# Two interleaved attention layers on one core: P transposed over 80 columns, P.V in whole-array matmuls, the row load moved into mid-step, the local layer's weights loaded in step one, and shorter last steps

## The chip, the cores and the metric

The kernel runs on one core of one Trainium2 chip. The metric is device time in microseconds (us) of one execution; lower is better. Engines are named as the profile names them: PE (matmuls), PEld (loads of the stationary operand into PE), DVE (vector), ACT (scalar), POOL (GpSimd) and SP (which here only issues DMAs; its queue is SPq).

## What is computed

Two layers, A and B, are applied one after the other, and then both again to the result. `x` has 2048 rows of 640 features.

```python
x = x + A(layernorm(x)); x = x + B(layernorm(x))
x = x + A(layernorm(x)); x = x + B(layernorm(x))

def A(x):                                   # 32 heads of 192, segments of 32 rows
    mem = mem0                              # 8 rows
    for s in range(64):
        h = concat([mem, x[32*s:32*s + 32]])          # 40 rows
        q, k, v = h @ Wq, h @ Wk, h @ Wv              # per head
        p = softmax(where(mask, q @ k.T / sqrt(192), -1e9))
        o = (p @ v) @ Wo
        mem, out_s = o[:8], o[8:]                     # memory goes on to the next segment

def B(x):                                   # 32 heads of 20, window of 8 keys, every second row back
    q, k, v = split(x @ wqkv)
    attn = softmax(where(pos - 2*w >= 0, q . k[pos - 2*w] / sqrt(20), -1e9))
    return (sum_w attn * v[pos - 2*w]) @ wo
```

In layer A each segment needs the memory of the segment before it, so the segments follow one another.

## The kernel before

**Steps.** The two passes run together. In step s, layer A works on segment s of the first pass (l = 0) and on segment s - 2 of the second (l = 1): 2 x 40 = 80 rows that share each weight. The local layer B works one step behind on the same two passes. There are 67 steps, 0 to 66: layer A runs in steps 0 to 65, layer B in steps 1 to 66. In steps 65 and 66 nothing is left of the first pass for layer B, and before the change its half is computed all the same.

**Weights.** Layer A's weights come in 64 pieces of 480 KB, called halves: 32 for q and k, 16 for v, 16 for the output. 31 stay in SBUF. The other 33 are streamed again in every step through a ring of 5 buffers (`half`, L216): in step 0 from the inputs, with a copy laid out for later written to DRAM by POOL's queue (L227), and from step 1 on from that copy (L230), in two DMAs of 240 KB, 66 in a step. All are issued by SP in the order in which PE uses the halves, and one is issued only when the half that had its buffer five loads earlier has been used.

**The order within a step** is written out by hand in `ORDER` (L53): each word is a call. PE and SP keep exactly this order (`manual_schedule`, L532); for DVE, ACT and POOL a scheduler decides the order when the program is built, and each engine then runs its own list in that order.

- `q` i (L295): q and k of two heads in 60 matmuls of 80 columns; ACT copies the result (L310).
- `v` i (L339): v of two heads in 5 matmuls of 384 columns; DVE copies the odd ones (L362), ACT the even ones (L360), into vt.
- `s` g (L312): scores of a group of 8 heads: 16 matmuls on 64x64 tiles of the array and 16 on 128x64 tiles. On DVE: mask (L330), maximum (L332), subtraction (L333); the exponential on ACT (L334); then on DVE sum (L336), reciprocal (L337) and product (L338), which gives P, the tile Pm.
- `t` g (L341): four transposes of Pm on PE (L345); DVE and ACT copy one half of the partitions each into PT (L347, L348).
- `pv` g (L365): P.V of the group on 128x64 tiles: 24 matmuls (L373), two tiles at a time; ACT copies the result (L376).
- `o` j (L379): the output projection, added up over the whole step in two accumulators (L390).
- For layer B: `ln1` (L418), `qkv` (L424; the products of q and k on DVE for l = 0 and on POOL for l = 1, L445), `logits` (L448, on 128x32 tiles; its softmax L465 to L473 ends with attn), `e` c (L477: PE spreads attn, DVE multiplies, L483, and adds up, L485), `wo` (L487) and `ln2` (L505).

At the end of a step `finish_step` (L393) has DVE copy the new memory into the next step's input (ST, L401); the next `q0` waits for it.

**Rows of x.** Every four steps 128 rows are loaded (`input_load`, L239), normalized on DVE and ACT (bst L249, L250, lnst, xn L254) and transposed by PE (`input_tile`, L243). The load is issued as steps 1, 5, 9, ... begin (L549), the transposes stand at `input0` in the step after. `store` (L512) writes 128 finished rows every four steps.

**Local weights.** wqkv (2400 KB) and wo (800 KB) are loaded whole as step 0 begins, ahead of all halves (L545).

Of the kernel before, what the change touches and what calls it, by code (L numbers as in the profile page):

```python
# [45 lines left out]
LAG = 2  # L46
# [4 lines left out]


ORDER = """  # L53
q0 v0 q1 ln10 alpha0 q2 v1 input0 q3 v2 s0 q4 qkv0 v3 t0 q5 q6 v4 q7 v5 logits0
s1 pv0 q8 o0 o1 v6 q9 e0 t1 v7 q10 o2 o3 e1 q11 v8
s2 pv1 q12 e2 o4 o5 v9 q13 e3 t2 v10 o6 o7 q14 e4 v11 q15 v12
s3 pv2 wo0 o8 v13 v14 ln20 t3 v15 store0 o9 o10 pv3 o11 o12 o13 o14
"""


def stages():

    names = ("alpha", "ln1", "qkv", "logits", "input", "wo", "ln2", "store", "pv", "q", "s", "t", "v", "o", "e")
# [43 lines left out]
class Kernel:  # L107
# [108 lines left out]
    def half(self, h):  # L216
# [123 lines left out]

    def p_transpose(self, g):  # L341
        nc = self.nc
        ps = self.ps.tile([P, 4, 2, SLOT], BF16, name="pt_ps", tag="ps")
        for j in range(4):
            nc.tensor.transpose(out=ps[:, j, :, :].rearrange("p h q -> p (h q)"),  # L345
                                in_=self.Pm[g % 2][:, j, :, :].rearrange("p l t -> p (l t)"), identity=self.ident[:, :])
        nc.vector.tensor_copy(out=self.PT[g % 2][0:64, :, :, 0, :], in_=ps[0:64, :, :, 0:LT])  # L347
        nc.scalar.copy(out=self.PT[g % 2][64:128, :, :, 1, :], in_=ps[64:128, :, :, 0:LT])  # L348

    def v(self, i):  # L350
        nc = self.nc
# [10 lines left out]
            nc.vector.tensor_copy(out=vt[:, :], in_=ps[:, :])  # L362
        self.vts[i] = vt

    def pv(self, g):  # L365
        nc = self.nc
        for k in (2 * g, 2 * g + 1):
            ps = self.ps.tile([P, 2, 3, 2, LT], F32, name="o_ps", tag="ps")
            for jj in range(2):
                i = 2 * k + jj  # L370
                vt = self.vts.pop(i)
                for (n, slot, h, col) in ((0, 0, 0, 0), (0, 1, 0, 64), (1, 0, 0, 128), (1, 1, 1, 192), (2, 0, 1, 256), (2, 1, 1, 320)):
                    nc.tensor.matmul(ps[64 * slot:64 * (slot + 1), jj, n, :, :], lhsT=vt[:, col:col + 64], rhs=self.PT[g % 2][:, i % 4, h, :, :],  # L373
                                     start=True, stop=True, tile_position=(0, 64 * slot))
# [40 lines left out]
        self.xr_next = xr  # L415


    def b_stats(self):  # L418
        self.bs = self.ln_stats(self.xr[:, :, :, :].rearrange("p c l t -> p c (l t)"), 2 * SEG)
        xn = self.w1.tile([P, NCH, 2 * SEG], BF16, name="xnB", tag="n")  # L420
        self.ln_apply(self.xr[:, :, :, :].rearrange("p c l t -> p c (l t)"), *self.bs, xn[:, :, :], 2 * SEG)
        self.xnB = xn

    def b_qkv(self):  # L424
        nc = self.nc
        qT = self.w1.tile([P, NCH, 2, SEG], BF16, name="qT", tag="q")
        kh = self.w2.tile([P, NCH, 2, BPAD + SEG], BF16, name="kh")
        vh = self.w2.tile([P, NCH, 2, BPAD + SEG], BF16, name="vh")
        for new, old in ((kh, self.kh), (vh, self.vh)):
            if old is None:  # L430
                nc.gpsimd.memset(new[:, :, :, 0:BPAD], 0.0)
            else:
                nc.gpsimd.tensor_copy(out=new[:, :, :, 0:BPAD], in_=old[:, :, :, SEG:SEG + BPAD])
        for kind, dst in enumerate((qT[:, :, :, :], kh[:, :, :, BPAD:], vh[:, :, :, BPAD:])):
            ps = self.ps.tile([P, NCH, 2, SEG], F32, name="qkv_ps", tag="ps")
            for d in range(NCH):
                for c in range(NCH):
                    nc.tensor.matmul(ps[:, d, :, :], lhsT=self.wqkv[:, c, kind * D + d * P:kind * D + (d + 1) * P],  # L438
                                     rhs=self.xnB[:, c, :].rearrange("p (l t) -> p l t", l=2), start=(c == 0), stop=(c == NCH - 1))
            nc.scalar.copy(out=dst, in_=ps[:, :, :, :])  # L440
        self.qT, self.kh, self.vh = qT, kh, vh
        self.prod = self.w1.tile([P, NCH, 2, BW, SEG], BF16, name="prod")
        for l in range(2):
            eng = nc.vector if l == 0 else nc.gpsimd
            eng.tensor_tensor(out=self.prod[:, :, l, :, :], in0=qT[:, :, l, :].unsqueeze(2).to_broadcast([P, NCH, BW, SEG]),  # L445
                              in1=window(kh, l), op=ALU.mult)

    def b_logits(self):  # L448
        nc = self.nc
        hf = SEG // 2  # L450
        ps = self.ps.tile([P, BW, hf], F32, name="lg_ps", tag="ps")
# [24 lines left out]

    def b_expand(self, c):  # L477
        nc = self.nc
        ps = self.ps.tile([P, 2, BW, SEG], F32, name="bc_ps", tag="ps")
        nc.tensor.matmul(ps[:, :, :, :].rearrange("p l w t -> p (l w t)"), lhsT=self.ET[:, c, :],  # L480
                         rhs=self.attn[:, :, :, :, :].rearrange("p l w h t -> p (l w h t)"), start=True, stop=True)
        pv = self.prod[:, c, :, :, :]
        nc.vector.tensor_tensor(out=pv, in0=ps[:, :, :, :], in1=window1(self.vh, c), op=ALU.mult)  # L483
        with nc.allow_low_precision("bf16 result of an f32 sum"):
            nc.vector.tensor_reduce(out=self.oT[:, c, :].rearrange("p (l t) -> p l t", l=2), in_=pv.rearrange("p l w t -> p l t w"), op=ALU.add, axis=AX.X)  # L485

    def b_wo(self):  # L487
        nc, s = self.nc, self.step
        ps = self.ps.tile([P, NCH, 2, SEG], F32, name="y_ps", tag="ps")
        for d in range(NCH):  # L490
            for c in range(NCH):
                nc.tensor.matmul(ps[:, d, :, :].rearrange("p l t -> p (l t)"), lhsT=self.wo[:, c, d * P:(d + 1) * P], rhs=self.oT[:, c, :],  # L492
                                 start=(c == 0), stop=(c == NCH - 1))
        if s <= self.n_seg:
            x2 = self.w2.tile([P, NCH, SEG], BF16, name="x2")
# [29 lines left out]
    def run(self):  # L525
# [6 lines left out]
        with tc.manual_schedule(engines={PE, SP}):  # L532
# [86 lines left out]
```

## Time and profile before

| | |
|---|---|
| Median of 3 runs | 3517.87 us (3513.82 to 3522.08) |
| The profiled execution | 3520.67 us, its span 3519.0 us |
| DVE, ACT, POOL busy | 62%, 42%, 11% of the span |
| Step 0 (first q0 matmul to that of step 1) | 128.9 us |
| Steps 4 to 61, mean by s mod 4 = 0, 1, 2, 3 | 52.22, 50.62, 51.83, 51.09 us |
| From the last q0 (step 65, at 3438.3) to the end | 80.7 us |
| Read from DRAM, written | 1091.7 MB, 18.8 MB |

The profile's page gives busy times and what each group of instructions waited for. The costliest groups on the lines that the change touches (line, engine, operation, output from input, shapes, count; then busy time and the mean of one; then idle time just before, and what ended it):

```profile
L373 PE MATMUL o_ps<-PT,vt 128*64 128x80 bf16 x6336 | 161.1, 203 | 0.5 <-issue 0.4
L345 PE MATMUL pt_ps<-ident,Pm 128*128 128x128 bf16 x1056 | 103.6, 221 | 0.6 <-issue 0.3 <-DVE Pm L338 0.2
L347 DVE COPY PT<-pt_ps 64x320 bf16<-64x320 bf16 x264 | 80.7, 306 | 15.0 <-PE pt_ps L345 15.0
L485 DVE TENSOR_REDUCE oT<-prod 128x64 bf16<-128x512 bf16 x330 | 336.7, 1021 | 4.5
```

A matmul's duration of some 200 ns is its latency: many are under way at once. What one costs in a stream is read from the distance between the starts, or from the chain of waits. The timeline gives start and length of each instruction, with equal neighbours merged (x15), and for an engine that stood idle, for how long and what ended it.

### The profile page before, as it was taken

How to read it: one execution, taken by the hardware profiler on the slowest of the kernel's cores; microseconds unless marked ns; L12 is line 12 of the kernel's file. 1: busy time of each engine (PE TensorE's matmuls, PEld its weight loads, DVE VectorE, ACT ScalarE, POOL GpSimd, SP SyncE). 2: the span in 40 equal slices, each digit the busy share in tenths (PEclk: the TensorE clock that was granted, in tenths of full speed). 3: DMA queues.
4: the chain of work that ended last, by engine and by line, in shares of the span. 5: the costliest groups of instructions: out<-in, count | busy, mean ns of one | idle time of the engine just before them, and what ended most of it. 6: DMA issues, size and time to landing. Idle time of an engine off the chain costs nothing.

```text
span 3519.0 us, 172521 instructions
## 1 busy us (share of the span) xinstructions
PE 3388.8 (96%) x78044; PEld 2891.7 (82%) x78045; DVE 2197.2 (62%) x5056; ACT 1479.6 (42%) x3213; POOL 369.9 (11%) x467
## 2 busy tenths in 40 slices
PE   5799999999999999999999999999999999999997
PEld 3588888888888888888888888888888888888886
DVE  1366666666666666666666666666666666666665
ACT  1244444444444444444444444444444444444443
POOL 2110110010111011001101101110010111011000
PEclk7799999999999999999999999999999999999998
DMA  9999999999999999999999999999999999999995
GB/s 350 352 321 320 318 320 315 316 320 323 319 323 317 317 314 322 320 322 319 322 326 322 324 322 320 318 324 326 321 319 323 315 320 324 320 317 319 319 320 202
DMA packets 664961, 1121.84 MB, mean 319 GB/s; under 512 B 70744, under 2 KB 661472, under 8 KB 664224
## 3 DMA queue, kind: packets, MB, share of 16 engines
q1 hardware_dynamic: 659280, 1091.96, 92.5%
q0 software_dynamic: 2640, 16.22, 1.1%
q8 instruction: 610, 9.99, 1.1%
q10 hardware_dynamic: 2304, 2.62, 0.2%
q14 instruction: 127, 1.04, 0.1%
HBM read 1091.68 MB, written 18.84 MB: 316 GB/s over the span
## 4 chain that ended last, share of the span: by engine, by line
PE 83%; DMA 9%; DVE 4%; ACT 2%; SPq 1%; issue 1%; ACTq 0%; POOLq 0%; POOL 0%; DVEq 0%
PE qk_ps L308 29%; PE v_ps L356 21%; PE acc L390 13%; DMA wt<-Wr 4%; PE qkv_ps L438 4%; PE o_ps L373 3%; PE s_ps L326 3%; PE s_ps L320 3%; PE qk_ps L303 2%; PE bc_ps L480 2%; DMA x_sb<-in_A_x_dram 2%; PE pt_ps L345 1%; DMA wt<-in_A_Wv_dram 1%; SPq L214 1%; PE y_ps L492 1%
## 5 line engine op out<-in xcount | busy, mean ns | idle before, releaser
L310 ACT CAST QK<-qk_ps 128x480 bf16<-128x480 f32 x1056 | 581.5, 557 | 1042.7 <-PE qk_ps L308 828.5
L356 PE MATMUL v_ps<-wt,ST 128*128 128x384 bf16 x3630 | 717.4, 328 | 13.9 <-DMA wt<-in_A_Wv_dram 9.2
L308 PE MATMUL qk_ps<-ST,wt 128*128 128x80 bf16 x14850 | 687.8, 203 | 22.6 <-DMA wt<-in_A_Wq_dram 10.6
L308 PE MATMUL qk_ps<-ST,res 128*128 128x80 bf16 x14850 | 691.4, 202 | 18.1 <-DMA res<-in_A_Wq_dram 9.4
L308 PEld LDWEIGHTS <-wt 128*128 128x128 bf16 x14850 | 610.1, 100 | 78.8 <-DMA wt<-in_A_Wq_dram 11.8
L356 PEld LDWEIGHTS <-ST 128*128 128x128 bf16 x5280 | 466.1, 99 | 246.6 <-issue 16.4
L308 PEld LDWEIGHTS <-res 128*128 128x128 bf16 x14850 | 610.9, 100 | 48.9 <-DMA res<-in_A_Wq_dram 10.4
L390 PE MATMUL acc<-ot,res 128*128 128x80 bf16 x9900 | 465.6, 202 | 17.4 <-DMA res<-in_A_Wo_dram 9.6
L390 PEld LDWEIGHTS <-res 128*128 128x128 bf16 x9900 | 409.9, 100 | 38.3 <-DMA res<-in_A_Wo_dram 11.8
L362 DVE CAST vt<-v_ps 128x384 bf16<-128x384 f32 x528 | 290.2, 550 | 210.0 <-PE v_ps L356 209.8
L483 DVE TENSOR_TENSOR prod<-bc_ps,vh 128x512 bf16<-128x512 f32 x330 | 227.3, 689 | 245.0 <-PE bc_ps L480 244.4
L360 ACT CAST vt<-v_ps 128x384 bf16<-128x384 f32 x528 | 253.7, 481 | 244.8 <-PE v_ps L356 243.2
L485 DVE TENSOR_REDUCE oT<-prod 128x64 bf16<-128x512 bf16 x330 | 336.7, 1021 | 4.5
L356 PE MATMUL v_ps<-res,ST 128*128 128x384 bf16 x1650 | 326.8, 329 | 2.7 <-DMA res<-in_A_Wv_dram 2.7
L390 PE MATMUL acc<-ot,wt 128*128 128x80 bf16 x5940 | 309.9, 202 | 6.2 <-DMA wt<-in_A_Wo_dram 3.5
L376 ACT CAST ot<-o_ps 128x480 bf16<-128x480 f32 x528 | 268.4, 559 | 109.3 <-PE o_ps L373 109.3
L330 DVE TENSOR_TENSOR sb<-s_ps,maskA 128x320 f32<-128x320 f32 x264 | 129.7, 491 | 253.7 <-PE s_ps L326 253.6
L390 PEld LDWEIGHTS <-wt 128*128 128x128 bf16 x5940 | 261.3, 100 | 18.1 <-issue 4.7
L445 POOL TENSOR_TENSOR prod<-qT,kh 128x1280 bf16<-128x1280 bf16 x66 | 169.9, 2575 | 653.0 <-ACT kh L440 653.0
L348 ACT COPY PT<-pt_ps 64x320 bf16<-64x320 bf16 x264 | 110.9, 420 | 296.7 <-DVE PT L347 295.1
L273 POOL TENSOR_TENSOR sq<-x 128x160 f32<-128x160 bf16 x64 | 28.9, 452 | 1837.4 <-DVE x L496 1837.4
L445 DVE TENSOR_TENSOR prod<-qT,kh 128x1280 bf16<-128x1280 bf16 x66 | 201.2, 3048 | 3.4 <-ACT kh L440 3.4
(117 smaller groups left out, 3709.3 us busy)
## 6 DMA issues: line engine op xcount, KB each, us to landing
wt<-Wr SPq DMA_DIRECT2D x4290, 240.0 KB, 4.8
Wr<-wt POOLq DMA_DIRECT2D x33, 480.0 KB, 6.7
wt<-in_A_Wv_dram SPq DMA_DIRECT2D x11, 480.0 KB, 10.5
res<-in_A_Wo_dram SPq DMA_DIRECT2D x10, 480.0 KB, 10.8
wt<-in_A_Wk_dram SPq DMA_DIRECT2D x9, 480.0 KB, 11.1
res<-in_A_Wq_dram SPq DMA_DIRECT2D x9, 480.0 KB, 11.3
res<-in_A_Wk_dram SPq DMA_DIRECT2D x7, 480.0 KB, 10.2
wt<-in_A_Wq_dram SPq DMA_DIRECT2D x7, 480.0 KB, 10.2
```

The lines of the kernel that those rows point to most:

```text
L308: nc.tensor.matmul(ps[:, m, :, :], lhsT=w[m // 3][:, c, (m % 3) * P:(m % 3 + 1) * P], rhs=st[:, c, :, 0:LT], start=(c == 0), stop=(c == NC ...
L310: nc.scalar.copy(out=self.QK[i % NQK][:, 0:12 * LT], in_=ps[:, :, :, :].rearrange("p m l t -> p (m l t)"))
L330: nc.vector.tensor_tensor(out=sb[:, :, :], in0=sv, in1=self.maskA[:, :].unsqueeze(1).to_broadcast([P, 8, LT]), op=ALU.add)
L356: nc.tensor.matmul(ps[:, :], lhsT=st[:, c, :, :].rearrange("p l t -> p (l t)"), rhs=w[:, c, :], start=(c == 0), stop=(c == NCH - 1))
L360: nc.scalar.copy(out=vt[:, :], in_=ps[:, :])
L362: nc.vector.tensor_copy(out=vt[:, :], in_=ps[:, :])
L376: nc.scalar.copy(out=ot[:, :, :, :], in_=ps[:, :, :, :, :].rearrange("p j n l t -> p (j n) l t"))
L390: nc.tensor.matmul(a[:, at, :, :], lhsT=w[h][:, m, dc * P:(dc + 1) * P], rhs=self.ots[h // 2][:, 3 * (h % 2) + m, :, :], start=(h == 0 and ...
L438: nc.tensor.matmul(ps[:, d, :, :], lhsT=self.wqkv[:, c, kind * D + d * P:kind * D + (d + 1) * P], rhs=self.xnB[:, c, :].rearrange("p (l t) ...
L445: eng.tensor_tensor(out=self.prod[:, :, l, :, :], in0=qT[:, :, l, :].unsqueeze(2).to_broadcast([P, NCH, BW, SEG]), in1=window(kh, l), op=A ...
L483: nc.vector.tensor_tensor(out=pv, in0=ps[:, :, :, :], in1=window1(self.vh, c), op=ALU.mult)
L485: nc.vector.tensor_reduce(out=self.oT[:, c, :].rearrange("p (l t) -> p l t", l=2), in_=pv.rearrange("p l w t -> p l t w"), op=ALU.add, axi ...
```

## The change

- P is transposed by an ordinary matmul with the identity matrix, of which only the 80 columns that are used are moved; the result is float32 in PSUM.
- P.V is in two calls. `pm` (pv_main) does features 0 to 127 of the first head and the last 128 columns for the second in whole-array matmuls of 128 features, 8 in a group; `pt` (pv_tail) does the remaining 64 features of each head on 128x64 tiles, 8 in a group. In groups 0 to 2 `pm` stands ahead of the next group's scores and `pt` behind them.
- The row load is a word of its own, `load0`, after `t0` in steps 2, 6, 10, ..., and `input0` stands after `v9` of the same step.
- wqkv and wo are loaded in step 1, in five chunks each, ahead of q0 to q4 and of q8 to q12.
- In steps 65 and 66 layer B computes the second pass alone; in step 66 the product that POOL had is done by DVE.

```diff
-q0 v0 q1 ln10 alpha0 q2 v1 input0 q3 v2 s0 q4 qkv0 v3 t0 q5 q6 v4 q7 v5 logits0
-s1 pv0 q8 o0 o1 v6 q9 e0 t1 v7 q10 o2 o3 e1 q11 v8
-s2 pv1 q12 e2 o4 o5 v9 q13 e3 t2 v10 o6 o7 q14 e4 v11 q15 v12
-s3 pv2 wo0 o8 v13 v14 ln20 t3 v15 store0 o9 o10 pv3 o11 o12 o13 o14
+q0 v0 q1 ln10 alpha0 q2 v1 q3 v2 s0 q4 qkv0 v3 t0 load0 q5 q6 v4 q7 v5 logits0
+pm0 s1 pt0 q8 o0 o1 v6 q9 e0 t1 v7 q10 o2 o3 e1 q11 v8
+pm1 s2 pt1 q12 e2 o4 o5 v9 input0 q13 e3 t2 v10 o6 o7 q14 e4 v11 q15 v12
+pm2 s3 pt2 wo0 o8 v13 v14 ln20 t3 v15 store0 o9 o10 pm3 pt3 o11 o12 o13 o14
...
+    def local_weights(self, i):
+
+        if i < NCH:
+            self.nc.sync.dma_start(out=self.wqkv[:, i, :], in_=self.B_wqkv[i * P:(i + 1) * P, :])
+        elif 8 <= i < 8 + NCH:
+            self.nc.sync.dma_start(out=self.wo[:, i - 8, :], in_=self.B_wo[(i - 8) * P:(i - 7) * P, :])
...
     def p_transpose(self, g):
-        ps = self.ps.tile([P, 4, 2, SLOT], BF16, name="pt_ps", tag="ps")
+        ps = self.ps.tile([P, 4, 2, LT], F32, name="pt_ps", tag="ps")
         for j in range(4):
-            nc.tensor.transpose(out=ps[:, j, :, :].rearrange("p h q -> p (h q)"),
-                                in_=self.Pm[g % 2][:, j, :, :].rearrange("p l t -> p (l t)"), identity=self.ident[:, :])
+            nc.tensor.matmul(ps[:, j, :, :], lhsT=self.Pm[g % 2][:, j, :, :].rearrange("p l t -> p (l t)"), rhs=self.ident[:, :].rearrange("p (h t) -> p h t", h=2)[:, :, 0:LT],
+                             start=True, stop=True)
...
-    def pv(self, g):
+    def pv_main(self, g):
+        self.ops = []
         for k in (2 * g, 2 * g + 1):
             ps = self.ps.tile([P, 2, 3, 2, LT], F32, name="o_ps", tag="ps")
             for jj in range(2):
                 i = 2 * k + jj
-                vt = self.vts.pop(i)
-                for (n, slot, h, col) in ((0, 0, 0, 0), (0, 1, 0, 64), (1, 0, 0, 128), (1, 1, 1, 192), (2, 0, 1, 256), (2, 1, 1, 320)):
-                    nc.tensor.matmul(ps[64 * slot:64 * (slot + 1), jj, n, :, :], lhsT=vt[:, col:col + 64], rhs=self.PT[g % 2][:, i % 4, h, :, :],
-                                     start=True, stop=True, tile_position=(0, 64 * slot))
+                for n, h in ((0, 0), (2, 1)):
+                    nc.tensor.matmul(ps[:, jj, n, :, :], lhsT=self.vts[i][:, P * n:P * (n + 1)], rhs=self.PT[g % 2][:, i % 4, h, :, :],
+                                     start=True, stop=True)
+            self.ops.append(ps)
+
+    def pv_tail(self, g):
+        for k, ps in zip((2 * g, 2 * g + 1), self.ops):
+            for jj in range(2):
+                i = 2 * k + jj
+                vt = self.vts.pop(i)
+                for h in range(2):
+                    hs = slice(SLOT * h, SLOT * (h + 1))
+                    nc.tensor.matmul(ps[hs, jj, 1, :, :], lhsT=vt[:, P + SLOT * h:P + SLOT * (h + 1)], rhs=self.PT[g % 2][:, i % 4, h, :, :],
+                                     start=True, stop=True, tile_position=(0, SLOT * h))
...
+    def layers(self):
+
+        return (0, 1) if self.step <= self.n_seg else (1,)
...
-        for l in range(2):
-            eng = nc.vector if l == 0 else nc.gpsimd
+        for l in self.layers():
+            eng = nc.vector if l == 0 or self.step > self.n_seg + LAG - 1 else nc.gpsimd
...
     def b_expand(self, c):
+        ls = slice(self.layers()[0], 2)
...
-        nc.tensor.matmul(ps[:, :, :, :].rearrange("p l w t -> p (l w t)"), lhsT=self.ET[:, c, :],
-                         rhs=self.attn[:, :, :, :, :].rearrange("p l w h t -> p (l w h t)"), start=True, stop=True)
+        nc.tensor.matmul(ps[:, ls, :, :].rearrange("p l w t -> p (l w t)"), lhsT=self.ET[:, c, :],
+                         rhs=self.attn[:, ls, :, :, :].rearrange("p l w h t -> p (l w h t)"), start=True, stop=True)
...
-                if s == 0:
-                    nc.sync.dma_start(out=self.wqkv[:], in_=self.B_wqkv.rearrange("(c p) n -> p c n", p=P))
-                    nc.sync.dma_start(out=self.wo[:], in_=self.B_wo.rearrange("(c p) n -> p c n", p=P))
                 self.x2 = self.x2_next
-                if s % 4 == 1 and 4 * (s // 4 + 1) < self.n_seg:
-                    self.input_load(s // 4 + 1)
                 for what, i in PLAN:
+                    if s == 1 and what == "q":
+                        self.local_weights(i)
...
+                    elif what == "load" and s % 4 == 2 and 4 * (s // 4 + 1) < self.n_seg:
+                        self.input_load(s // 4 + 1)
                     elif what == "input" and s % 4 == 2 and 4 * (s // 4 + 1) < self.n_seg:
                         self.input_tile(s // 4 + 1)
```

More of the change, by code (lines that the diff above doesn't have):

```diff
@@ L53 @@
 ORDER = """
-q0 v0 q1 ln10 alpha0 q2 v1 input0 q3 v2 s0 q4 qkv0 v3 t0 q5 q6 v4 q7 v5 logits0
-s1 pv0 q8 o0 o1 v6 q9 e0 t1 v7 q10 o2 o3 e1 q11 v8
-s2 pv1 q12 e2 o4 o5 v9 q13 e3 t2 v10 o6 o7 q14 e4 v11 q15 v12
-s3 pv2 wo0 o8 v13 v14 ln20 t3 v15 store0 o9 o10 pv3 o11 o12 o13 o14
+q0 v0 q1 ln10 alpha0 q2 v1 q3 v2 s0 q4 qkv0 v3 t0 load0 q5 q6 v4 q7 v5 logits0
+pm0 s1 pt0 q8 o0 o1 v6 q9 e0 t1 v7 q10 o2 o3 e1 q11 v8
+pm1 s2 pt1 q12 e2 o4 o5 v9 input0 q13 e3 t2 v10 o6 o7 q14 e4 v11 q15 v12
+pm2 s3 pt2 wo0 o8 v13 v14 ln20 t3 v15 store0 o9 o10 pm3 pt3 o11 o12 o13 o14
 """
 def stages():
-    names = ("alpha", "ln1", "qkv", "logits", "input", "wo", "ln2", "store", "pv", "q", "s", "t", "v", "o", "e")
+    names = ("alpha", "ln1", "qkv", "logits", "load", "input", "wo", "ln2", "store", "pm", "pt", "q", "s", "t", "v", "o", "e")
     plan = []
@@ L342, in p_transpose @@
         nc = self.nc
-        ps = self.ps.tile([P, 4, 2, SLOT], BF16, name="pt_ps", tag="ps")
+        ps = self.ps.tile([P, 4, 2, LT], F32, name="pt_ps", tag="ps")
         for j in range(4):
-            nc.tensor.transpose(out=ps[:, j, :, :].rearrange("p h q -> p (h q)"),
-                                in_=self.Pm[g % 2][:, j, :, :].rearrange("p l t -> p (l t)"), identity=self.ident[:, :])
-        nc.vector.tensor_copy(out=self.PT[g % 2][0:64, :, :, 0, :], in_=ps[0:64, :, :, 0:LT])
-        nc.scalar.copy(out=self.PT[g % 2][64:128, :, :, 1, :], in_=ps[64:128, :, :, 0:LT])
+            nc.tensor.matmul(ps[:, j, :, :], lhsT=self.Pm[g % 2][:, j, :, :].rearrange("p l t -> p (l t)"), rhs=self.ident[:, :].rearrange("p (h t) -> p h t", h=2)[:, :, 0:LT],
+                             start=True, stop=True)
+        nc.vector.tensor_copy(out=self.PT[g % 2][0:64, :, :, 0, :], in_=ps[0:64, :, :, :])
+        nc.scalar.copy(out=self.PT[g % 2][64:128, :, :, 1, :], in_=ps[64:128, :, :, :])
     def v(self, i):
@@ L453, in b_logits @@
             for r in range(4):
-                nc.tensor.matmul(ps[32 * r:32 * (r + 1), :, :], lhsT=self.E[:, c, :], rhs=self.prod[:, c, r // 2, :, hf * (r % 2):hf * (r % 2 + 1)],
+                nc.tensor.matmul(ps[32 * r:32 * (r + 1), :, :], lhsT=self.E[:, c, :], rhs=self.prod[:, c, max(r // 2, self.layers()[0]), :, hf * (r % 2):hf * (r % 2 + 1)],
                                  start=(c == 0), stop=(c == NCH - 1), tile_position=(0, 32 * r))
@@ L478, in b_expand @@
         nc = self.nc
+        ls = slice(self.layers()[0], 2)
         ps = self.ps.tile([P, 2, BW, SEG], F32, name="bc_ps", tag="ps")
[L480 to L483 removed]
+        nc.tensor.matmul(ps[:, ls, :, :].rearrange("p l w t -> p (l w t)"), lhsT=self.ET[:, c, :],
+                         rhs=self.attn[:, ls, :, :, :].rearrange("p l w h t -> p (l w h t)"), start=True, stop=True)
+        pv = self.prod[:, c, ls, :, :]
+        nc.vector.tensor_tensor(out=pv, in0=ps[:, ls, :, :], in1=window1(self.vh, c, ls), op=ALU.mult)
         with nc.allow_low_precision("bf16 result of an f32 sum"):
[L485 removed]
+            nc.vector.tensor_reduce(out=self.oT[:, c, :].rearrange("p (l t) -> p l t", l=2)[:, ls, :], in_=pv.rearrange("p l w t -> p l t w"), op=ALU.add, axis=AX.X)
     def b_wo(self):
         nc, s = self.nc, self.step
+        ls = slice(self.layers()[0], 2)
         ps = self.ps.tile([P, NCH, 2, SEG], F32, name="y_ps", tag="ps")
@@ L491, in b_wo @@
             for c in range(NCH):
-                nc.tensor.matmul(ps[:, d, :, :].rearrange("p l t -> p (l t)"), lhsT=self.wo[:, c, d * P:(d + 1) * P], rhs=self.oT[:, c, :],
+                nc.tensor.matmul(ps[:, d, ls, :].rearrange("p l t -> p (l t)"), lhsT=self.wo[:, c, d * P:(d + 1) * P], rhs=self.oT[:, c, SEG * ls.start:],
                                  start=(c == 0), stop=(c == NCH - 1))
@@ L537, in run @@
             n_steps = self.n_seg + LAG
-            attend = {"q": self.qk, "s": self.scores, "t": self.p_transpose, "v": self.v, "pv": self.pv, "o": self.o}
+            attend = {"q": self.qk, "s": self.scores, "t": self.p_transpose, "v": self.v, "pm": self.pv_main, "pt": self.pv_tail, "o": self.o}
             local = {"ln1": self.b_stats, "qkv": self.b_qkv, "logits": self.b_logits, "wo": self.b_wo, "ln2": self.beta_x, "store": self.store}
```

5 lines of the change are left out of this document (3 added, 2 removed).

## Prediction

> **What bounds the kernel now.** I read the page's busy times and granted clock first, then the chain of waits and the timeline of step 45 (2410.25 to 2460.47 us, the first q0 matmul of one step to that of the next), then the waits by releaser.
>
> ```profile
> PE 3388.8 (96%) x78044; PEld 2891.7 (82%) x78045; DVE 2197.2 (62%) x5056; ACT 1479.6 (42%) x3213; POOL 369.9 (11%) x467
> PEclk7799999999999999999999999999999999999998
> ```
>
> PE is busy 96% of the span at full clock outside step 0. In the chain (start, length in us) nearly every piece of step 45 is PE work:
>
> ```profile
> 2427.92 0.36 PE s_ps L320 x16
> 2428.28 0.36 PE s_ps L326 x16
> 2428.64 0.44 PE o_ps L373 x24
> 2429.08 1.18 PE qk_ps L308 x30
> ...
> 2433.44 0.22 PE pt_ps L345 x4
> ```
>
> A step with no stall takes 50.2 us (step 45); the mean of steps 8 to 59 is 51.44. Of the 1.22 above the floor, 0.21 is work that only every fourth step has (row and output transposes, 0.56 + 0.28), 0.25 the wait shown last below, and about 0.76, 49 us in all, short waits for streamed weights. So PE is first, the weight stream is close behind (DMA share 0.97 in step 45), and what makes PE wait counts in full.
>
> **Transposes.** 4 in 0.22 us, 56 ns each at 128 columns; 80-column matmuls take 36 ns each (30 in 1.07). The change saves 264 x 4 x 20 ns = 21.1 us. The product now comes out in float32: DVE's copy PT (306 ns, L347) has no such row; a plain bf16 copy is the low end, the 128x384 float32 cast (550, L362) scaled to 320 elements the high one, 0.46. I take 0.46, as it too casts from PSUM; it is hidden, since pm3, the tightest, runs 1.5 us after t3 and the copies need 1.1.
>
> **P.V.** 24 half-array matmuls, run in pairs, take 0.44, or 36.7 ns a pair. Per head pair three such pairs become two whole matmuls (36) and one pair: 4 x 108 ns = 0.43. Nothing is gained. The price of changing the array's shape is in the row after o_ps: 1.18 instead of 1.07, 0.1 us. Groups 1 to 3 change shape as often as before; group 0 goes from logits (32-column tiles) to whole to scores, once more than before: 65 x 0.1 = +6.5 us.
>
> **What the new order does to DVE.** The whole matmuls of P.V now stand ahead of the next scores (pm0 s1 pt0), so scores 1, 2 and 3 end 0.29 us later (0.39 for s1, with the change of shape), while the transposes that need their Pm keep their places. DVE's queue in the changed build is also reordered. Group 1 before:
>
> ```profile
> 2428.68 0.49 DVE L330 TENSOR_TENSOR sb<-s_ps,maskA 128x320 f32<-128x320 f32 x1
> 2429.09 0.37 DVE L469 TENSOR_REDUCE smb<-sbb 128x16 f32<-128x128 f32 x1
> 2430.29 1.17 DVE L473 TENSOR_TENSOR attn<-sbb,smb 32x128 bf16<-32x128 f32 x4
> 2432.25 0.49 DVE L338 TENSOR_TENSOR Pm<-sb,sm 128x320 bf16<-128x320 f32 x1
> 2433.28 0.39 PE L345 MATMUL pt_ps<-ident,Pm 128*128 128x128 bf16 x4
> ```
>
> Pm ends 2432.74, t1 starts 2433.28: 0.49 to spare, with 0.05 for the semaphore. Afterwards smb stands ahead of sb, and attn ahead of the subtraction (L333), so that the exponential (0.47 on ACT), which ran under attn, is waited for. Queue from 2429.08, start to start: smb 0.29, sb 0.41, reciprocal 0.16, mx 0.39, attn 1.09, subtraction 0.51, exponential 0.54, sum 0.52, reciprocal 0.23, Pm 0.49: it ends at 2433.71, and t1 wants it at 2433.33. Wait: 0.38. In group 2 one product moves under the exponential; Pm ends about when it did (2444.0): no wait. Group 3:
>
> ```profile
> 2454.44 0.48 DVE L338 TENSOR_TENSOR Pm<-sb,sm 128x320 bf16<-128x320 f32 x1
> 2454.84 0.55 DVE L362 CAST vt<-v_ps 128x384 bf16<-128x384 f32 x1
> 2454.97 0.40 PE L345 MATMUL pt_ps<-ident,Pm 128*128 128x128 bf16 x4
> ```
>
> Here PE starts 0.05 after Pm: no slack at all. Afterwards the vt cast stands ahead of Pm, and scores come 0.29 later. Starts: mask add 2451.62, mx 2452.14, subtraction 2452.67, exponential (ACT) 2453.19, sum 2453.69, ssq 2454.10, reciprocal 2454.40, vt 2454.51, Pm 2454.98: it ends 2455.46, wait about 0.57. Behind t1 and t3 stand all of PE's later instructions. 65 x (0.38 + 0.57) = +61.8 us; bounds 0.2 (scores shift alone, nothing from the order) to 1.2 a step, 13 to 78.
>
> **Row load.** Before, it is issued as step 1, 5, ... begins, and DVE waits for it ahead of finish_step:
>
> ```profile
> 345.84 0.38 SPq L241 DMA_DIRECT2D x_sb<-in_A_x_dram  x1
> ...
> 350.59 0.89 DVE L249 BATCH_NORM_STATS2 bst<-x_sb 128x6 f32<-128x320 bf16 x2 [1.31 <-DMA x_sb<-in_A_x_dram]
> ...
> 352.87 0.20 DVE L401 CAST ST<-acc 128x48 bf16<-128x48 f32 x1
> ```
> ```profile
> PE qk_ps L303 <- DVE ST L401: 14.4, 14, 1.8
> ```
>
> That goes: -14.4 us. In the changed build SP has the load behind streamed half 35 (the 15th and 16th of a step's 66 issues) in steps 2, 6, ... 58, 15 times, and DVE has the first bst ahead of the scores of group 0. SP can't issue half 35 before q2 frees a buffer: in step 34 (from 1846.84) at 1851.46, +4.6, so the row load goes at +5.4. Half 35's time to landing:
>
> ```profile
> wt<-Wr SPq DMA_DIRECT2D x2, 240.0 KB, 4.4
> ```
>
> The row loads of before took 4.9 in the median. So it lands at +9.9 (9.4 to 10.6), while scores 0 are ready at +8.0 and t0 stands at +12.0, as in the steps 3, 7, ... Behind bst on DVE wait the mask add and the whole softmax; within it now also the second bst (0.49), the aggregate (0.21), the scalar op, which also waits for ACT (about 0.3), and xn (0.45). From landing: first bst 0.5, then 5.0 where the chain took 3.4 (L330 to the end of Pm). Pm ends at +15.4, t0 waits 3.4 us (3.0 to 4.1): 15 x 3.4 = +51 us.
>
> Such a gap also lowers the clock. Windows of 3.4 us in step 0 (length, PE busy, then the other engines', granted clock, DMA share, GB/s):
>
> ```profile
> 34.71:38.12 3.41, 1.55 (x51) 1.34 (x51) 1.95 (x4) 0.95 (x2) 0.54 (x1) 1.00 1.03 351
> 38.12:41.54 3.42, 2.10 (x19) 1.42 (x19) 0.70 (x3) 0.56 (x1) 1.08 (x2) 0.50 1.04 398
> 62.02:65.43 3.41, 1.81 (x44) 1.54 (x42) 1.72 (x5) 1.50 (x4) 0.00 (x0) 1.00 1.10 390
> 65.43:68.84 3.41, 0.91 (x17) 0.71 (x18) 0.00 (x0) 0.00 (x0) 0.00 (x0) 1.00 1.03 351
> ```
>
> After a window with 1.55 busy the clock is 0.50; after 1.81 it stays. So over about 1.85 idle in one window halves the next. A 3.4 us gap leaves that much in one of its two windows in some nine cases of ten, and then one or two windows run at half speed: by where the gap falls, 0 to 2.6 us lost, mean 1.7: 15 x 1.7 = +25.5. The Trainium skill ("TensorE: Matmul & The Clock Gate", Part 1) has the clock fall only after a window that is idle altogether; by that the gap would almost never cost clock, and the sum would be 25 lower. The rows above, none of them idle, speak against it.
>
> **Local weights.** 3.28 MB leave step 0, where DMA share is above 1 at 350 to 400 GB/s: -9 us. In step 1 five chunks of 480 KB stand among the first seven streamed halves; at 1.35 us each (365 GB/s, about the mean of step 0), counted from the last load of step 0, 2.8 us before step 1 begins, half 9 lands at 12 x 1.35 - 2.8 = +13.4, and q4 wants it at +8.0: +5.5. Net -3.5 (bounds -9 to +1). qkv0 waits for nothing more, since its last chunk is issued ahead of half 8.
>
> **Last step.** The chain has 7.8 us for five products and sums (L483, L485); at half the width a pair costs about 0.9 instead of 1.55: -3.3. The logits product leaves POOL (3.06 in the chain) for DVE, without the other layer's beside it: about -1.4. Together -4.7 (-3 to -6).
>
> **Relief.** PE's new waits let the ring fill. Of the 49 us that PE waits for streamed weights I give back 30 (0 to 49): nearly all in the steps with the long wait and a bit of the next, half elsewhere.
>
> **Sum.** -21.1 + 6.5 + 61.8 - 14.4 + 51 + 25.5 - 3.5 - 4.7 - 30 = +71 on the profiled execution's 3520.67 us (span 3519.0 and 1.67 around it): 3592. The median of the runs is 2.8 lower: 3589, say 3590, slower by 2%.
>
> **Rivals.** (1) The clock holds, by the rule that only an idle window lowers it: 3590 - 25 = 3565. For it: nothing in steady state ever fell; against: the windows above. 0.13. (2) Groups 1 and 3 are not late, because DVE in fact has more room than one stall-free step shows: 3590 - 62 + 20 less relief = 3548. For it: a weight wait of PE ahead of t1 or t3 would give DVE time; against: t3 has 0.05 to spare. 0.13. (3) The other side: DVE is never late. Place: its queue from scores to Pm. The row load, a third smaller than a half's part, would have to land by +6.5, when DVE is done with v1, and the reordered queue to fit its slack. Then what is left is -21.1 + 6.5 - 14.4 - 3.5 - 4.7 = -37, of which about 12 go back to weight waits: 3520.7 - 25 - 2.8 = 3493. It decides at a landing 1.1 us after issue; the rows have 4.4 to 4.9. 0.12. My forecast has 0.62.
>
> **Numbers.** A change under 0.2%, 7 us, can't be told from none. Slower: 0.62 + 0.13 + 0.13 less a little: 0.87; same 0.02; faster 0.11. Own bounds of the forecast: 45 to 62 for t0, 0 to 39 for the clock, 13 to 78 for t1 and t3, 0 to 49 of relief; rivals 1 and 2 lie inside. Range 3530 to 3640.
>
> **What would show it.** Right: pt_ps waits for DVE Pm some 15 times 3 to 4 us, and at t1 and t3 of nearly every step 0.3 to 0.6; bst waits for x_sb 15 times for over 2 us; granted clock 0.50 for a window or two after each; four transposes in 0.14; o_ps together still 0.43; waits for ST L401 gone. Wrong: Pm waits absent, then rival 3; clock 1.00 behind the gaps, rival 1; a row load that lands in 2 us.

## The result, and the profile after

| | before | after |
|---|---|---|
| Median of 4 runs each, us | 3516.49 (3513.82 to 3522.08) | 3627.06 (3624.56 to 3628.57) |
| Ratio | 1 | 1.0312 (95% interval 1.0294 to 1.0329) |
| Profiled execution, its span | 3520.67, 3519.0 | 3627.75, 3626.1 |
| Step 0, step 1 | 128.94, 52.96 | 121.10, 57.96 |
| Steps 2 to 64 together | 3240.0 | 3356.3 |
| From the last q0 to the end | 80.64 | 74.28 |
| Shortest steps (after: with the waits at t1 and t3) | 50.2 | 51.08 |
| Steps 2 to 63, mean length by s mod 4 = 0, 1, 2, 3 | 52.22, 50.62, 51.83, 51.05 | 51.63, 51.26, 58.68, 51.44 |
| Half clock after step 1, up to 3400 us | 0 | 81.9 |

The kernel is 3.1% slower, 110.6 us. Both ends of the program gain (steps 0 and 1 together 3 us, the end 6), and the middle loses 116, most of it in the steps with s mod 4 = 2, those with the row load. The changed kernel's lines are numbered 7 to 24 higher: the transposes are L352, Pm is L345, the row load L248, bst L256, the products of q and k L468.

The page's busy times and granted clock, and the first line of its chain:

```profile
PE 3421.1 (94%) x75933; PEld 2915.3 (80%) x75933; DVE 2228.0 (61%) x5055; ACT 1489.2 (41%) x3213; POOL 371.1 (10%) x466
PEclk7799999999999999999999999999999999999999
PE 70%; DVE 16%; DMA 9%; ACT 2%; issue 1%; SPq 1%; POOL 0%; DVEq 0%; POOLq 0%; ACTq 0%
```

DVE's share of the chain was 4% before (PE 83%). The line of the clock shows nothing of the loss: 81.9 us at half clock are 2% of the span, and each of the 40 slices rounds them off. The waits, first PE's, then DVE's for the rows (us in total, times, longest):

```profile
PE pt_ps L352 <- DVE Pm L345: 114.5, 128, 5.6
PE qk_ps L315 <- DMA wt<-Wr: 11.2, 25, 1.2
```
```profile
DVE bst L256 <- DMA x_sb<-in_A_x_dram: 63.3, 16, 4.9
```

The first group is new; it was 0.2 before. The wait of q0 for ST is gone. This is a step with a row load, step 34, which begins at 1902.67 (timeline: start, length, engine, instruction; in brackets the idle time before and what ended it):

```profile
1908.19 0.38 SPq L248 DMA_DIRECT2D x_sb<-in_A_x_dram  x1
...
1913.02 0.49 DVE L256 BATCH_NORM_STATS2 bst<-x_sb 128x6 f32<-128x320 bf16 x1 [3.74 <-DMA x_sb<-in_A_x_dram]
1913.43 0.47 DVE L337 TENSOR_TENSOR sb<-s_ps,maskA 128x320 f32<-128x320 f32 x1
...
1913.89 0.98 PE L363 MATMUL v_ps<-wt,ST 128*128 128x384 bf16 x5
...
1916.53 2.59 POOL L468 TENSOR_TENSOR prod<-qT,kh 128x1280 bf16<-128x1280 bf16 x1 [12.36 <-ACT kh L463]
1916.72 2.74 DVE L345 TENSOR_TENSOR Pm<-sb,sm 128x320 bf16<-128x320 f32 x1
...
1919.39 0.92 DVE L468 TENSOR_TENSOR prod<-qT,kh 128x1280 bf16<-128x1280 bf16 x1
1919.53 0.45 PE L352 MATMUL pt_ps<-ident,Pm 128*128 128x80 bf16 x4 [4.66 <-DVE Pm L345]
```

The load goes at +5.5 us of the step, DVE takes up the rows at +10.35 (10.67 on average over the 15 such steps), and PE, done with v3 at +12.2, stands until +16.86. One row was not foreseen: Pm, 0.49 elsewhere, takes 2.74 here and in each of the 15 steps, about as long as POOL's product beside it. And what follows the gap (windows: length; PE, PEld, DVE, ACT, POOL busy; granted clock; DMA share; GB/s):

```profile
1912.28:1915.69 3.41, 2.59 (x66) 2.00 (x62) 2.20 (x6) 0.92 (x4) 0.00 (x0) 1.00 0.94 301
1915.69:1919.10 3.41, 0.00 (x0) 0.00 (x0) 3.35 (x5) 1.09 (x5) 2.57 (x2) 1.00 0.89 317
1919.10:1922.52 3.42, 3.00 (x46) 3.00 (x47) 2.07 (x4) 0.93 (x2) 1.37 (x3) 0.50 0.02 6
1922.52:1925.93 3.41, 3.41 (x62) 2.63 (x59) 0.00 (x0) 1.65 (x4) 0.00 (x0) 1.00 0.77 240
```

One window has PE idle, the next one runs at half clock, and in it next to no weights move (6 GB/s), as the ring has filled in the meantime. The clock falls in 15 of 15 such steps, for one window or two. In the other groups the late Pm looks like this, group 3 of step 44:

```profile
2485.68 0.20 DVE L344 RECIPROCAL sm<-sm 128x8 f32<-128x8 f32 x1
2485.79 0.51 DVE L369 CAST vt<-v_ps 128x384 bf16<-128x384 f32 x1
...
2486.21 0.48 DVE L345 TENSOR_TENSOR Pm<-sb,sm 128x320 bf16<-128x320 f32 x1
...
2486.75 0.32 PE L352 MATMUL pt_ps<-ident,Pm 128*128 128x80 bf16 x4 [0.42 <-DVE Pm L345]
```

The vt cast stands between the reciprocal and Pm, and PE waits. Brackets count idle from matmul ends that are modelled, so from here on a wait is taken as the distance from the start of the matmul ahead to that of the transpose, less the usual distance: the means are 0.34 us at t1, 0.57 at t3, 0 at t2, and 4.99 at t0 in the steps with a row load.

### The profile page after: what moved, and what is told of

It reads as the page before. It is cut to its first block, busy times and chain, and to the rows that moved or that the text cites. A ratio compares the mean times of both kernels' runs of the same rounds, so it can differ in the third digit from the quotient of the medians.

```text
span 3626.1 us, 168317 instructions
## 1 busy us (share of the span) xinstructions
PE 3421.1 (94%) x75933; PEld 2915.3 (80%) x75933; DVE 2228.0 (61%) x5055; ACT 1489.2 (41%) x3213; POOL 371.1 (10%) x466
## 4 chain that ended last, share of the span: by engine, by line
PE 70%; DVE 16%; DMA 9%; ACT 2%; issue 1%; SPq 1%; POOL 0%; DVEq 0%; POOLq 0%; ACTq 0%
PE qk_ps L315 24%; PE v_ps L363 18%; PE acc L409 13%; DMA wt<-Wr 5%; DVE Pm L345 3%; PE qkv_ps L461 2%; DMA x_sb<-in_A_x_dram 2%; PE qk_ps L310 2%; PE s_ps L333 2%; PE s_ps L327 2%; DVE sb L340 2%; ACT sb L341 2%; PE o_ps L380 2%; PE pt_ps L352 2%; DVE sb L337 2%; PE bc_ps L504 2%
## 5 line engine op out<-in xcount | busy, mean ns | idle before, releaser
L315 PE MATMUL qk_ps<-ST,wt 128*128 128x80 bf16 x14850 | 701.6, 205 | 22.6 <-DMA wt<-Wr 11.2
L315 PE MATMUL qk_ps<-ST,res 128*128 128x80 bf16 x14850 | 701.9, 204 | 10.8 <-DMA res<-in_A_Wq_dram 6.4
L315 PEld LDWEIGHTS <-wt 128*128 128x128 bf16 x14850 | 624.4, 102 | 78.6 <-DMA wt<-Wr 17.2
L315 PEld LDWEIGHTS <-res 128*128 128x128 bf16 x14850 | 620.8, 102 | 40.3 <-DMA res<-in_A_Wq_dram 7.6
L409 PEld LDWEIGHTS <-res 128*128 128x128 bf16 x9900 | 410.8, 100 | 33.7 <-DMA res<-in_A_Wo_dram 11.2
L509 DVE TENSOR_REDUCE oT<-prod 128x64 bf16<-128x512 bf16 (+1 forms) x330 | 331.6, 1005 | 4.5
L507 DVE TENSOR_TENSOR prod<-bc_ps,vh 128x512 bf16<-128x512 f32 (+1 forms) x330 | 224.8, 682 | 169.1 <-PE bc_ps L504 164.7
L409 PEld LDWEIGHTS <-wt 128*128 128x128 bf16 x5940 | 264.1, 100 | 17.3 <-DMA wt<-in_A_Wo_dram 4.5
L355 ACT CAST PT<-pt_ps 64x320 bf16<-64x320 f32 x264 | 111.2, 421 | 369.7 <-DVE PT L354 368.0
L468 POOL TENSOR_TENSOR prod<-qT,kh 128x1280 bf16<-128x1280 bf16 x65 | 167.9, 2583 | 688.4 <-ACT kh L463 688.4
L352 PE MATMUL pt_ps<-ident,Pm 128*128 128x80 bf16 x1056 | 84.6, 206 | 114.8 <-DVE Pm L345 114.5
```

The costliest lines, as they stand in the source:

```text
L315: nc.tensor.matmul(ps[:, m, :, :], lhsT=w[m // 3][:, c, (m % 3) * P:(m % 3 + 1) * P], rhs=st[:, c, :, 0:LT], start=(c == 0), stop=(c == NC ...
L352: nc.tensor.matmul(ps[:, j, :, :], lhsT=self.Pm[g % 2][:, j, :, :].rearrange("p l t -> p (l t)"), rhs=self.ident[:, :].rearrange("p (h t) ...
L409: nc.tensor.matmul(a[:, at, :, :], lhsT=w[h][:, m, dc * P:(dc + 1) * P], rhs=self.ots[h // 2][:, 3 * (h % 2) + m, :, :], start=(h == 0 and ...
L507: nc.vector.tensor_tensor(out=pv, in0=ps[:, ls, :, :], in1=window1(self.vh, c, ls), op=ALU.mult)
```

## The experiments

Three terms of the prediction carry the result: the row load, what comes of its gap, and the two late groups. The first four kernels test them one by one. Medians and ranges are over 4 to 11 runs, ratios are to the kernel before on the same chip (its medians were 3517.3 to 3518.0), with 95% intervals. "Lower tenth" is the length that a tenth of the steps stay under.

**The row load at its old place (e1).**

```diff
-q0 v0 q1 ln10 alpha0 q2 v1 q3 v2 s0 q4 qkv0 v3 t0 load0 q5 q6 v4 q7 v5 logits0
+q0 v0 q1 ln10 alpha0 q2 v1 input0 q3 v2 s0 q4 qkv0 v3 t0 q5 q6 v4 q7 v5 logits0
...
+                if s % 4 == 1 and 4 * (s // 4 + 1) < self.n_seg:
+                    self.input_load(s // 4 + 1)
```

> The changed kernel with the row load and its transposes put back where they were (load as steps 1, 5, ... begin, transposes after v1 of the step after); all else as changed. My theory: 15 waits of 5.0 us at t0 and the half-clock windows behind them (82 us at half speed, some 30 lost) go, the old wait at the end of every fourth step (14 us) comes back, and some weight waits return (+10): 3627 - 75 - 32 + 14 + 10 = about 3545, the clock 1.00 from step 1 to step 65, waits at t1 and t3 as in the changed kernel (0.34 and 0.57). Rival, that the float32 transposes or P.V hold PE and the row load only shares their place: above 3600.

Measured: 3530.22 (3525.15 to 3532.6), ratio 1.0032 (1.0019 to 1.0044), 97 us below the changed kernel and 15 below what I had expected. Waits at t1 and t3 are as in the changed kernel (0.33, 0.56), t0 has none, and the clock stays at 1.00 from step 2 to step 65.

```profile
PE pt_ps L352 <- DVE Pm L345: 40.0, 106, 1.9
```

So 74.5 us of the 114.5 were t0's, 15 x 4.97, and the row load with what hangs on it is 97 of the 110.6 us. I had put 62 on it, relief aside.

**The whole matmuls behind the next scores (e2).** The order in groups 1 to 3 is `s1 pm0 pt0` and so on in place of `pm0 s1 pt0`.

> The changed kernel with pm put behind the next scores again, directly ahead of pt (s1 pm0 pt0, and so on), where P.V stood before; all else as changed. My theory: the waits at t1 and t3 (0.34 and 0.57 in each of 65 steps, 59 us) fall to 0.06 at most, and the additional change of the array's shape (6.5 us) goes; some 20 us return as weight waits: about 3580. The waits at t0 of every fourth step stay at 5 us. Rival, that whole-array P.V or the float32 copies cost the time themselves: 3620 or more.

Measured: 3597.71 (3593.41 to 3603.9), ratio 1.0229 (1.0202 to 1.0255), 29 us less. The waits at t1 and t3 are gone altogether (means 0.01 and 0.00), which settles their cause: the order of `pm` and the scores, with DVE's order that follows from it (how much each of the two does is not parted). That no more than 29 comes out of 65 x 0.91 = 59 us of waits has a second reason: PE now goes from scores on half the array to whole matmuls to half ones and back, five changes of shape more a step than the changed kernel. At the 0.1 us of the prediction they are 65 x 0.5 = 32 us, and 59 - 32 = 27. The lower tenth of the steps bears it out: 50.57 us against 51.08, only 0.51 less, though the two waits in such a step were 0.44 and 0.58.

**Both at their old places (e3).**

> Both of the above together: row load as before, pm directly ahead of pt behind the scores. Left of the change are the transposes over 80 columns (-21), P.V in whole-array matmuls (0), the local weights in step 1 (-3) and the short last steps (-6). My theory: faster than the kernel before by 20 to 30 us, about 3492, with weight waits taking back some 8. Rival, that something else in the change costs time too: 3517 or more. Second rival, that the weight stream sets the pace of every step: within 5 us of the kernel before.

Measured: 3507.56 (3501.18 to 3511.11), ratio 0.9972 (0.9959 to 0.9984): faster than before, by 10. No wait for Pm is left; PE's longest row of waits is again

```profile
PE qk_ps L310 <- DVE ST L420: 11.7, 11, 1.9
```

So the two moves are the whole loss. The gain is 15 us short of what I had expected, and the steps themselves show where it went: their lower tenth is 50.75 us where the kernel before has 50.32, though each has 0.32 us less of transposes. That is PE's own work and no wait; against the kernel before, this order has six more changes of the array's shape in a step. e6 below tests it.

**Both products of q and k on DVE (e4).** In step 34 of the changed kernel Pm lies under POOL's product. If that is the cause of its 2.74 us, taking the product from POOL frees it:

```diff
-            eng = nc.vector if l == 0 or self.step > self.n_seg + LAG - 1 else nc.gpsimd
+            eng = nc.vector
```

> The changed kernel with both products of q and k on DVE instead of one on POOL. In the steps with the row load DVE's Pm took 2.74 us instead of 0.49, while POOL's product ran. My theory: DVE's bf16 output waits while POOL works (a shared resource), so with POOL idle Pm takes 0.49 there, t0 waits 2.7 instead of 5.0, the products take some 0.9 each instead of 3.0, and fewer windows run at half clock: 3627 - 34 - 15 = about 3578. Rival, that Pm is long because of what it waits for on DVE and ACT: Pm still 2.7, the time 3625 or more, since DVE now has a second product.

Measured: 3580.48 (3571.91 to 3582.58), ratio 1.0174 (1.0147 to 1.02), 47 us less. Step 34 again, then the products in the view of their tile (ns, minimum/median/maximum):

```profile
1886.36 0.49 DVE L256 BATCH_NORM_STATS2 bst<-x_sb 128x6 f32<-128x320 bf16 x1 [4.11 <-DMA x_sb<-in_A_x_dram]
...
1890.07 0.58 DVE L345 TENSOR_TENSOR Pm<-sb,sm 128x320 bf16<-128x320 f32 x1
1890.58 1.65 DVE L468 TENSOR_TENSOR prod<-qT,kh 128x1280 bf16<-128x1280 bf16 x2
1890.71 0.32 PE L352 MATMUL pt_ps<-ident,Pm 128*128 128x80 bf16 x4 [2.87 <-DVE Pm L345]
```
```profile
L468 DVE TENSOR_TENSOR prod<-qT,kh x130: 812/917/924, 155.8 to 3564.8; 128x1280 bf16<-128x1280 bf16 x130
```

Pm is never above 0.59 us, and DVE does both products in 1.65, less than the 3.08 that one took beside POOL's. t0 waits 2.76 us in place of 4.99, and half clock falls from 81.9 to 27.3 us. So the 2.2 us that Pm took longer are DVE's wait for POOL; the 2.76 that are left at t0 are the late rows and the queue behind them. The Trainium skill ("SBUF — State Buffer", section "SBUF: two separate sides") states it as an exclusive lock: a DVE instruction with two SBUF inputs and a GpSimd instruction that reads SBUF don't share, and the one that starts first has the ports until it ends. The trace agrees: in the changed kernel POOL starts 0.19 us ahead, and Pm ends 0.34 after it. In e4 Pm meets a short POOL copy (at 1889.85, 0.46 us) and again ends 0.34 after it.

**Work in the gap, to part the wait from the clock (e8).** 110 matmuls whose result is not used stand ahead of t0 in the 15 steps; t0 itself can't start sooner.

```diff
+                    if what == "t" and i == 0 and s % 4 == 2 and 4 * (s // 4 + 1) < self.n_seg:
+                        ps = self.ps.tile([P, LT, 2], F32, name="fill", tag="ps")
+                        for _ in range(110):
+                            nc.tensor.matmul(ps[:, :, :].rearrange("p t l -> p (t l)"), lhsT=self.ident[:, :], rhs=self.ident[:, 0:2 * LT], start=True, stop=True)
```

> The changed kernel with 110 matmuls of the identity over 80 columns (about 4 us of PE, their result is not used) ahead of t0 in the 15 steps with a row load, where PE stands idle for 5 us. Theory, the gap lowers the clock and that costs some 25 to 40 us by itself: Pm is as late as before (t0 starts no later), the clock stays at 1.00, and the time falls from 3627 to about 3595. Rival, the half clock is hidden in the wait for weights or in the idle time itself: 3627 as before, with clock 1.00. Rival, the clock has another cause than idle PE: still half for 80 us, and 3627.

Measured: 3591.63 (3585.73 to 3593.86), ratio 1.0203 (1.0185 to 1.0222), 35 us below the changed kernel, with more work done. Step 34, then the windows around its gap:

```profile
1894.18 4.11 PE L577 MATMUL fill<-ident 128*128 128x80 bf16 x110
1896.04 2.75 DVE L345 TENSOR_TENSOR Pm<-sb,sm 128x320 bf16<-128x320 f32 x1
1898.85 0.32 PE L352 MATMUL pt_ps<-ident,Pm 128*128 128x80 bf16 x4 [0.56 <-DVE Pm L345]
```
```profile
1894.90:1898.31 3.41, 3.39 (x95) 3.25 (x91) 3.24 (x5) 1.19 (x5) 2.46 (x1) 1.00 0.66 230
1898.31:1901.73 3.42, 2.88 (x68) 2.69 (x69) 2.18 (x4) 1.18 (x3) 1.48 (x3) 1.00 0.13 30
```

Pm takes as long as it did and t0 starts 17.0 us into the step on average (17.2 in the changed kernel), the clock stays at 1.00 from step 2 to step 65, and so all but some 3 of the 35 us are the price of the lowered clock, 2.2 us a gap.

**PE's own work in the gap (e10).** In the same 15 steps t0 stands behind q5, q6 and v4; the row load keeps its place.

```diff
+                plan = list(PLAN)
+                if s % 4 == 2 and 4 * (s // 4 + 1) < self.n_seg:
+                    plan.remove(("t", 0))
+                    plan.insert(plan.index(("v", 4)) + 1, ("t", 0))
```

> The changed kernel with t0 moved behind v4 in the 15 steps with a row load: q5, q6 and v4, 3.3 us of PE, stand in what was the gap, and the load keeps its place. Theory: t0 waits 5.0 - 3.3 = 1.7 us, the clock stays at 1.00, and the time falls by 15 x 3.3 + 35 = 85 us less a third for weight waits, to 3560 at most and 3540 at least. Rival, the wait only moves on (logits for DVE's product, scores of group 1 behind it): some other wait of 3 us shows in the 15 steps, the clock falls still, and the time stays above 3590.

Measured: 3558.22 (3548.61 to 3564.36), ratio 1.011 (1.0092 to 1.0128), 69 us less than the changed kernel, four fifths of the 85. t0 waits 1.72 on average, nothing else waits in its place, and half clock is down to two windows in all, each behind a gap like this one:

```profile
1879.15:1882.56 3.41, 1.36 (x22) 0.84 (x21) 3.41 (x3) 1.37 (x4) 3.41 (x3) 1.00 1.05 382
1882.56:1885.97 3.41, 3.41 (x48) 2.22 (x44) 1.46 (x4) 0.98 (x2) 0.35 (x1) 0.50 0.66 215
```

**The transposes alone (e5).** The kernel before, with `p_transpose` of the changed one and nothing else.

> The kernel before, with one part of the change alone: the four transposes of a group are matmuls over 80 columns into float32. Theory: PE saves 264 x 0.08 = 21 us of its own work, a stall-free step falls by 0.3 us (50.3 to 50.0 in the lower tenth of the steps), but the stream of weights is close behind PE, and about two thirds of it come back as waits for weights: some 3510 us, 7 less than the kernel before, the mean step 0.1 us shorter. Rival, PE sets the pace and keeps it all: 3496. Rival, the float32 copy PT makes P.V late: slower than before, with waits for PT ahead of o_ps.

Measured: 3500.98 (3495.29 to 3512.15), ratio 0.995 (0.9933 to 0.9968), 17 us less (11 to 24 by the interval). My theory fell: most of the 21 us is kept, which is nearer to the rival. The lower tenth of the steps goes from 50.32 to 50.07. The float32 copy PT takes 0.47 us and no P.V waits for it.

**All but the split P.V and the row load (e6), and the same with the local weights in step 0 (e9).** e6 has `pv` as before (`s1 pv0` and so on, `pv3`) and the row load of e1; e9 takes out the call of `local_weights` as well and loads both whole in step 0.

> The changed kernel with the row load at its old place and P.V as before, in 24 half-array matmuls; the transposes, the local weights in step one and the short last steps stay. Theory: against the run with both parts put back, six changes of the array's shape a step are gone (0.1 us each, 0.6 a step, 39 us in all), the lower tenth of the steps goes from 50.75 to about 50.1; the weight stream takes half to three quarters of it back: 3490 to 3500 us, below both kernels. Rival, the split costs nothing at this place and only the weights set the pace: 3507, as the run with both put back. Rival, PE keeps all of it: 3470.

> The run without the split, with the local weights again loaded whole in step 0: the new transposes and the short last steps alone are left. Theory: step 0 goes back from 121 to 128 us and step 1 from 58 to 52, so 1 to 3 us slower than the run without the split, 3496 to 3500. Rival: the steps behind step 1, 7 us longer in the run without the split than with the transposes alone, were slowed by the late load: then 3488 to 3493.

Measured: e6 3494.74 (3484.73 to 3496.72), ratio 0.9922 (0.9904 to 0.994); e9 3492.65 (3482.63 to 3502.36), ratio 0.9923 (0.9903 to 0.9944). Both beat both kernels. From e3 to e6 the lower tenth of the steps falls from 50.75 to 50.20, 0.55 for the six changes of shape a step, as expected; of these 36 us 13 reach the end, and the rest must have gone to waits. Between e6 and e9 nothing can be told. In the profiles step 0 is 121 and 128 us, step 1 58.5 and 53.4, the steps 2 to 64 3224.3 and 3223.9: what step 0 gains, step 1 gives back but for 2 us. e9 was 3 to 7 us faster than I expected, at the rival's number, but the rival's reason, slower steps behind step 1, is not in the trace. What separates e9 from e5 are the short last steps: 8 us by the medians, on two chips and with intervals that overlap; in the profiles the time from the last q0 to the end is 7.5 us shorter (79.73 and 72.26).

**The row load after v12 of step 0, 4, 8, ... (e7),** an attempt to get rid of the ST wait in e6:

```diff
-s2 pv1 q12 e2 o4 o5 v9 q13 e3 t2 v10 o6 o7 q14 e4 v11 q15 v12
+s2 pv1 q12 e2 o4 o5 v9 q13 e3 t2 v10 o6 o7 q14 e4 v11 q15 v12 load0
```

> As the run without the split, but the row load is a word of its own after v12 of steps 0, 4, 8, ..., and its statistics stand on DVE behind the copy PT of group 2, with 4 us to the next scores, so that the waits for ST (11.7 us in the run with both put back) go. Theory: no wait of PE for ST or for Pm, bst waits about 1 us for the rows with nothing urgent behind it; 12 us less work on the path, a third of it kept: 4 us less than the run without the split. Rival: the rows land later than 4 us after DVE is there, the softmax of group 3 is late and t3 waits over 1 us in 15 steps: 15 us more.

Measured: 3510.07 (3504.84 to 3519.41), ratio 0.9986 (0.9971 to 1.0), 15 us more than e6. A miss, and the rival's number came about in another way: PE waits for Pm twice in the whole run, not in 15 steps. The ST wait went, but DVE stood 3 us for the rows, not 1, and what was behind it, which I had called not urgent, came late to PE in 14 to 16 steps each:

```profile
PE acc L397 <- ACT ot L383: 10.3, 14, 0.7
...
PE ln_ps L286 <- DVE ssq L282: 8.5, 15, 1.4
PE y_ps L505 <- DVE oT L497: 7.0, 16, 1.0
```
```profile
DVE bst L256 <- DMA x_sb<-in_A_x_dram: 47.0, 16, 3.6
```

## Why the prediction was right

The forecast was 3590, slower by 2%, in a range of 3530 to 3640; it is 3627. The case that was called likeliest is the one that happened: Pm late at t0, t1 and t3, with the clock lowered by the gap. Chains of kernels that differ in one part give each part its price, in us:

| Part | predicted | measured | from |
|---|---|---|---|
| Transposes | -21.1 | -17 | before to e5 |
| Last steps | -4.7 | -8 | e5 to e9 |
| Local weights | -3.5 | +2, not told from 0 | e9 to e6 |
| P.V: shape +6.5, t1 and t3 +61.8 | +68.3 | +35 | e6 to e1 |
| Row load: t0 +51, clock +25.5, ST -14.4 | +62.1 | +97 | e1 to after |
| Relief | -30 | within the rows above | |

The measured rows hold the relief of their part, the predicted ones don't. In the terms of the sum, t0 was 24 us too low (15 x 4.99 = 75, not 51), the clock 10 too low (35, not 25.5) and the relief 10 too high; the other terms are within 3. With these sizes, 59 for t1 and t3, what both ends of the program gained, and the transposes, the shape and ST as predicted, the terms add up to some 131 us ahead of the relief, of which 110.6 came through, so 20 us were given back and not 30. All three errors point the same way, and t0 lies outside its own bounds of 45 to 62. The forecast, +71 where +110.6 was measured, had the mechanism; that 3627 lies in the range is owed to its width.

- **t0.** The step "first bst 0.5, then 5.0" priced the queue of before, and left out that Pm would slide under POOL's product. From the first bst to the end of Pm it is 4.29 us in e4 and 6.45 in the changed kernel, in all 15 steps: without POOL my 5.5 was 1.2 too long, with it 0.9 too short. DVE also took up the rows at +10.67 on average, not +9.9. Wait: 4.99, not 3.4. The profile of before had the sign: the product took about 3.05 on DVE beside POOL's. The prediction allowed for it in the last step alone ("without the other layer's beside it") and did not ask what else would come to stand beside POOL's product.

```profile
L445 DVE TENSOR_TENSOR prod<-qT,kh 128x1280 bf16<-128x1280 bf16 x66 | 201.2, 3048 | 3.4 <-ACT kh L440 3.4
```

- **Clock.** 33 to 35 us by e8 where I had 25.5, for a gap of 5.0 us and not 3.4. The mechanism was that of the windows in step 0, but the limit of 1.85 us idle that I read there is not sharp (last section). Of the 15 windows ahead of a fall in the changed kernel, 8 had some matmuls in them, up to 0.91 us, and in e10 both had over 1.3. So the rule of the Trainium skill ("TensorE: Matmul & The Clock Gate", Part 1), that the clock falls after an idle window, doesn't cover these falls. That was rival 1.
- **t1 and t3.** 0.34 and 0.57, where 0.38 and 0.57 were worked out from DVE's new order. Rivals 2 and 3 fell: these groups are late, and the rows are taken up 5.1 us after the load is issued, not 1.1.
- **P.V and the shape.** Two whole matmuls and a pair cost what three pairs did: one of the shortest steps, in which t1 waits 0.44 and t3 0.58, went up by 0.88, and -0.32 + 0.1 + 0.44 + 0.58 leaves 0.08 for it. The 0.1 for a change of shape was borne out by e3 against e6, 0.55 for six.
- **Relief.** I gave back 30 over the whole sum. The kernels show it where PE's waits are many and short: of the +65 in P.V half was hidden in waits that PE had anyhow (q0 waits 12.1 us for ST in e6 and 4.5 in e1; the mean of steps 2 to 64 is 0.98 us above their lower tenth in e6 and 0.60 in e1); of the long gaps at t0 nearly all came through (15 x 4.99 and 35 for the clock, less the 4.5 that q0 waits for ST in e1, are 105; 97 were measured).
- **Last steps.** From the last q0 to the end 80.64 became 74.28, 6.4 less against 4.7.
- **Readings that change nothing in the sum.** 51.44 is the mean of steps 4 to 61 (steps 8 to 59: 51.40). The clock of the kernel before is at half for 25 us near the end of the program too, not in step 0 alone. A `q` call has 30 matmuls, as the prediction counts them, not the 60 of the description.

## What to carry over

A load that is moved closer to its use is paid for by every instruction that is queued behind its first reader on an in-order engine: follow that queue to what PE waits for, and see what the shifted instructions then lie beside. If an instruction's duration in a profile has another engine's work beside it, look for one without before using it as a price. When a gap on PE can't be closed, put independent matmuls from later in the step into it (e10): it saves the gap and the clock behind it.

## What the hardware showed that was not expected

- DVE waits while POOL works, where both read two tiles of SBUF: Pm 2.74 us beside POOL's product and 0.49 alone, the product of q and k about 3.08 beside POOL's and 0.92 without it. Two products one after the other on DVE (1.65) end sooner than one on each engine.
- The clock goes by windows of 3.41 us that need not be idle, and the PE time that the profile shows in one gives no sharp limit. In e10 it fell after windows with 1.36 and 1.40 us of PE work and in e5 once after 1.51 (1779.41); in e4 it outlived windows with 1.45 (206.49) and 1.54 (626.33), and in step 1 of the changed kernel it fell after one with 2.23 (147.58).
